# Reordering the start of a fused adaLN attention and MLP kernel: condition vector ahead of x, one PSUM bank per transposed chunk

## The chip, the cores and the metric

The kernel runs on one core of one Trainium2 chip. The metric is device time in microseconds (us) of one execution. The profile shows one execution: its span is counted from the first to the last instruction, and all times inside it are counted from the span's start. Engines: PE (matrix multiply; PEld is its weight load), DVE (vector), ACT (scalar, activations), POOL, and SP, which issues DMAs.

## The reference

One transformer block with adaptive layer norm, batch 1, 2048 tokens, width 512, 32 heads of 16, MLP width 1376, all inputs bfloat16:

```python
mod = (silu(c) @ w_mod).reshape(1, 6, 1, 512)   # c: condition vector, 512 values
sa, ca, ga, sb, cb, gb = mod[:, 0], ..., mod[:, 5]
h = layernorm(x) * (1 + ca) + sa
x = x + ga * attention(h, wqkv, wo)              # 32 heads, softmax over 2048 keys
h = layernorm(x) * (1 + cb) + sb
x = x + gb * (gelu(h @ w1 + b1) @ w2 + b2)
```

## The kernel before

The 2048 tokens are four blocks of 512 (`xb[0]` to `xb[3]`, each 4 token tiles of 128). A **prologue** handles block 0; then one long **attention stage** runs over 32 quads (a quad is four heads and one block of queries), into which the rest of the projections, the output projection and the MLP of finished blocks are woven. The order of the attention stage is written by a planner inside the kernel (jobs with due times, modelled engine clocks); the prologue is ordered by hand. The engines then run their instructions in that order, each held only by semaphores.

The prologue, by the lines that the change and the prediction touch:

- Loads. SP issues the first half of `xb[0]` (L138), ACT the second half (L138) and then the condition vector `cc_bf` (L139); each then issues half of the modulation weights `W_m0` (L128). `later_loads` (L143) puts the other loads on SP behind a trigger: a one-element memset on DVE (L145), placed behind the first statistics of block 0, into the destination of the first of these loads. The order there is W_k (first half), W_q (first half), `xb[1]`, W_v, `xb[2]`, `xb[3]` and the rest.
- `silu_c` (L196): one exponential on ACT (L198), three small operations on DVE (L199 to L201). It stands in DVE's order ahead of the layer-norm statistics of block 0 (`ln_stats`, L213, one per token tile).
- `warm_up` (L376): 18 matmuls on zeros that keep PE busy while x is loaded. Behind them `first_mod_mm` (L267): 32 matmuls of width 1 that make the modulation columns in `psm`.
- `ln1_norm` (L353): square root on ACT (L248), four normalisations on DVE (L253).
- Transposes (L258): 16 of 128x128, chunk by chunk of the width; a chunk j takes the same 128 columns of all four token tiles. Chunks 0 and 1 share one PSUM tile (a bank), chunks 2 and 3 another.
- `first_mod` (L282, L283) copies the modulation columns; `hT_evac` (L298 on DVE for chunks 0 and 2, L295 on ACT for chunks 1 and 3) scales, shifts and writes `hT`.
- `k_proj` (L303, four matmuls), `k_evac` on ACT (L309), `q_proj` (L317), then `ST1` = 3 statistics of block 1, then `q_evac` (L326): two operations on DVE that write the two halves of `qm`, for even and odd heads; the fourth statistic of block 1 is a planner's job and comes after it.

The attention stage reserves its PSUM banks after the prologue's pools are closed: two single banks `psX0`, `psX1` (name `aux`), one for the output of a quad (`od`), three for scores `sA`, two for scores `sB`. In the prologue the pools stood in the order: one bank for `psm`, two for the transposes, four for products (`ppj`), so that the query products lay in a bank that later belongs to `sA`. First in the stage come scores of quad 0 (L1019, `sA` and `sB`), two value products (L332), and the exponentials on ACT (L1071). Value products are evicted by ACT (L339). Matmuls on zeros (L1235, "fills") are put in by the planner where PE would have little to do. Layer norm of blocks 1 to 3 runs on DVE as jobs: four aggregations (L221), three small steps (L223 to L227), six newton steps (L235 to L238), four normalisations (L253); then transposes, evictions, and `k_proj` with an eviction on DVE (L311).

Of the kernel before, what the change touches and what calls it, by code (L numbers as in the profile page):

```python
# [12 lines left out]
BF16 = mybir.dt.bfloat16  # L13
FP32 = mybir.dt.float32
# [3 lines left out]
PSUM = bass.MemoryType.PSUM  # L18
DRAM = bass.MemoryType.DRAM

P = 128
# [4 lines left out]
NC = 4  # L26
# [24 lines left out]
PE_, ACT_, DVE_, POOL_, SP_ = range(5)  # L51
# [4 lines left out]
PE_LAT = 0.18  # L56
EXP = {1: 0.5, 2: 0.92, 3: 1.34}

ST1 = 3

WARM = 18

# [13 lines left out]
V_EVAC = 0.63  # L76
# [17 lines left out]
def adaln_block(ctx: ExitStack, tc: tile.TileContext, A_x, A_wqkv, A_wo, B_x, B_w1, B_b1, B_w2, B_b2,  # L94
                c, w_mod, out):
    nc = tc.nc
    x_tok = A_x[0].rearrange("(b t p) d -> b p t d", b=NQB, p=P)
# [8 lines left out]
    hT = res.tile([P, NC, S], BF16, name="hT")  # L106
# [13 lines left out]
    pron = pro.enter_context(tc.tile_pool(name="pron", bufs=2, side="right"))  # L120
# [3 lines left out]
    def load_mod(i, engs):  # L124
        t = prom.tile([P, NC, 2 * D], BF16, name="W_m")
        n = NC // len(engs)
        for k, eng in enumerate(engs):
            eng.dma_start(out=t[:, n * k:n * k + n, :], in_=wm_v[:, n * k:n * k + n, 2 * i * D:2 * (i + 1) * D])  # L128
        return t

    xb = [prox.tile([P, 4, D], BF16, name="xb") for _ in range(NQB)]
    cc_bf = const.tile([P, NC], BF16, name="cc_bf")
    W_k = prow.tile([P, NC, D], BF16, name="W_k")
    W_v = prow.tile([P, NC, D], BF16, name="W_v")

    two = (nc.sync, nc.scalar)
    for k, eng in enumerate(two):
        eng.dma_start(out=xb[0][:, 2 * k:2 * k + 2, :], in_=x_tok[0][:, 2 * k:2 * k + 2, :])  # L138
    nc.scalar.dma_start(out=cc_bf, in_=c.rearrange("o (p j) -> p (o j)", j=NC))  # L139
    W_m0 = load_mod(0, two)  # L140
    mods = {}

    def later_loads():  # L143

        nc.vector.memset(W_k[0:1, 0, 0:1], 0.0)  # L145
        nc.sync.dma_start(out=W_k[:, :, 0:256], in_=wqkv_v[:, :, D:D + 256])
        nc.sync.dma_start(out=W_q[:, :, 0:256], in_=wqkv_v[:, :, 0:256])
        nc.sync.dma_start(out=xb[1], in_=x_tok[1])
        nc.sync.dma_start(out=W_v, in_=wqkv_v[:, :, 2 * D:3 * D])
        for b in range(2, NQB):  # L150
            nc.sync.dma_start(out=xb[b], in_=x_tok[b])
        nc.sync.dma_start(out=W_k[:, :, 256:D], in_=wqkv_v[:, :, D + 256:2 * D])
        nc.sync.dma_start(out=W_q[:, :, 256:D], in_=wqkv_v[:, :, 256:D])
        mods[1] = load_mod(1, (nc.sync,))
# [4 lines left out]
    ident = const.tile([P, P], BF16, name="ident")  # L159
# [52 lines left out]
    def ln_stats(src, st, t, i):  # L212
        nc.vector.bn_stats(out=st[:, i, :], in_=src[:, t, :])  # L213
# [42 lines left out]
    def transpose_chunk(ps, src, j, tiles):  # L256
        for i, t in enumerate(tiles):
            nc.tensor.transpose(out=ps[:, i * P:(i + 1) * P], in_=src[:, t, j * P:(j + 1) * P],  # L258
                                identity=ident)
# [17 lines left out]
    def first_mod_mm(ps):  # L277
        mod_cols(ps, W_m0, 0, 0)
        mod_cols(ps, W_m0, D, 4)
# [13 lines left out]
    def hT_evac(dst, ps, col, eng):  # L293
        if eng == "act":
            nc.scalar.activation(out=dst, in_=ps, func=ACT.Identity, bias=modc[:, col:col + 1],  # L295
                                 scale=modc[:, col + 4:col + 5])
        else:
            nc.vector.tensor_scalar(out=dst, in0=ps, scalar1=modc[:, col + 4:col + 5],  # L298
                                    scalar2=modc[:, col:col + 1], op0=ALU.mult, op1=ALU.add)
# [51 lines left out]
    hn_t = [None] * NQB  # L351

    def ln1_norm(b, st):  # L353

        mv, rs = ln_sqrt(st, 4)

        nc.scalar.activation(out=ce_x, in_=eps_c, func=ACT.Exp)
        for t in range(4):
            ln_norm(xb[b], xb[b], mv, rs, t, t)
        hn_t[b] = xb[b]  # L360

    with tc.tile_pool(name="pps", bufs=1, space=PSUM) as pps0, \
            tc.tile_pool(name="ppst", bufs=2, space=PSUM) as ppst, \
            tc.tile_pool(name="ppsm", bufs=4, space=PSUM) as ppsm:
        silu_c()
        st0 = pron.tile([P, 12, 6], FP32, name="st1")
        for t in range(4):
            ln_stats(xb[0], st0, t, t)
            if t == 0:
                later_loads()  # L370

        idle = ppsm.tile([P, 512], FP32, name="ppj")

        def warm_up(n):
            for _ in range(n):
                nc.tensor.matmul(out=idle, lhsT=warm[:, 0:P], rhs=warm, start=True, stop=True)  # L376
        warm_up(WARM)
        psm = pps0.tile([P, 16], FP32, name="psm")
        ln1_norm(0, st0)
        pt_ = [ppst.tile([P, 2, 512], BF16, name="ptr") for _ in range(2)]  # L380
        first_mod_mm(psm)
        for j in range(NC):
            transpose_chunk(pt_[j // 2][:, j % 2, :], hn_t[0], j, range(4))
        first_mod(psm)
        for j in range(NC):
            hT_evac(hT[:, j, 0:512], pt_[j // 2][:, j % 2, :], j, "act" if j % 2 else "dve")
        ps = ppsm.tile([P, 512], FP32, name="ppj")
        k_proj(ps, 0, 0)
        k_evac(ps, 0, 0, "act")
        ps = ppsm.tile([P, 512], FP32, name="ppj")  # L390
        q_proj(ps, 0, 0)
        st1 = pron.tile([P, 12, 6], FP32, name="st1")
        for t in range(ST1):
            ln_stats(xb[1], st1, t, t)
        q_evac(ps, 0, 0)

# [29 lines left out]
    lab = {}  # L426
# [13 lines left out]
    def job(at, rows, needs=(), label=None, hold=-1):  # L440
        jobs.append(Job(at, rows, needs, label, hold))

    lab[("k", 0, 0)] = lab[("q", 0, 0)] = lab[("x", 0)] = 0.0
    st_of = {1: st1}
    V_ENG = ["act"] * 9 + ["dve", "act", "dve", "dve", "act", "dve", "dve"]

# [56 lines left out]
    for b in range(1, NQB):  # L503
        at = 0.25 * (b - 1)
        def stats(j, b=b, t=0):
            if b > 1 and t == 0:
                st_of[b] = pron.tile([P, 12, 6], FP32, name="st1")
            ln_stats(xb[b], st_of[b], t, t)
        job(at - 0.16, [(DVE_, V_EVAC, lambda j, b=b, t=t, f=stats: f(j, b, t)) for t in range(ST1 if b == 1 else 0, 4)],
            [("n", b - 1)] if b > 1 else [], ("st", b))  # L510
        job(at - 0.1, ln_rows(b, lambda b=b: xb[b], lambda b=b: xb[b], "n"), [("st", b)], ("n", b))
        for j in range(NC):
            h_job(at, b, j)
        k_job(at + 0.01, 0, b)
        if b == 1:
            for kt in range(4):
                v_job(0.02, kt)
# [917 lines left out]
    while pv["q"] < nq or od_copy or jobs or active:  # L1435
        q = next_quad[0] - 1
# [50 lines left out]
```

## Time and profile before

| what | value |
|---|---|
| runs | 819.32, 817.38, 819.41 us; median 819.32 |
| profiled execution | 815.8 us, span 814.0 us |
| busy share of the span | PE 95%, ACT 93%, DVE 89%, POOL 9% |
| condition vector | issued 1.26, landed 5.80 |
| first layer-norm statistics (DVE) | 6.56 |
| warm-up block on PE | 2.68 to 9.55 |
| transposes of block 0 | 10.37 to 12.24 |
| block 1 of x | issued 8.26, landed 13.46 |
| query eviction | 15.28 to 16.68 |
| first scores, first exponential | 16.82, 17.31 |

The busy shares are means over stages with different limits. In the views, a line gives the start, the length, the engine, the line of the kernel, the operation, what it writes and reads, and in brackets how long its engine sat idle before it and what ended that wait. The chain view follows the work back from the last instruction of a stretch to what released it.

### The profile page before, as it was taken

The page shows a single profiled execution, that of the slowest core. Times are in us where ns is not written, and L with a number is a line of the kernel's source. Part 1 is how long each engine was busy: PE and PEld are TensorE (multiplying, and loading weights), DVE is VectorE, ACT ScalarE, POOL GpSimd, SP SyncE. Part 2 cuts the span into 40 slices and gives each one's busy share as a digit, 9 for nine tenths or more (in the row PEclk, how much of TensorE's full clock was granted, in tenths as well). Part 3 has the DMA queues.
Part 4 walks back from the last instruction along what each step waited for, and adds up shares of the span by engine and source line. Part 5 has one row for each costly group of instructions (what it writes and reads, how often), then busy time and mean ns, then how long its engine had stood idle before and what let it go on. Part 6 is the DMA issues. An engine that isn't in the chain of part 4 may idle for free.

```text
span 814.0 us, 18164 instructions
## 1 busy us (share of the span) xinstructions
PE 771.9 (95%) x7404; PEld 237.5 (29%) x7470; DVE 723.8 (89%) x1306; ACT 756.2 (93%) x681; POOL 71.2 (9%) x62
## 2 busy tenths in 40 slices
PE   7999999989999999999999999999999999999997
PEld 3432222322223222222222322222222222222254
DVE  7879989999998998998998999988998999889663
ACT  4898999989998999999999999999999999999962
POOL 0000000024000000101100000011100000011100
PEclk9999999999999999999999999999999999999999
DMA  8100000104100000001100000010100000010100
GB/s 269 68 1 16 15 16 15 42 16 140 41 15 16 15 17 2 14 23 29 48 16 16 16 10 8 14 29 21 48 15 16 15 3 15 15 28 23 48 2 29
DMA packets 30426, 24.49 MB, mean 30 GB/s; under 512 B 13473, under 2 KB 24194, under 8 KB 30338
## 3 DMA queue, kind: packets, MB, share of 16 engines
q1 hardware_dynamic: 29650, 22.49, 9.6%
q8 instruction: 60, 0.98, 0.5%
q10 hardware_dynamic: 688, 0.79, 0.3%
q14 instruction: 28, 0.23, 0.1%
HBM read 20.65 MB, written 2.61 MB: 29 GB/s over the span
## 4 chain that ended last, share of the span: by engine, by line
PE 46%; ACT 24%; DVE 17%; issue 10%; DMA 2%; SPq 0%; POOL 0%; ACTq 0%; DVEq 0%; POOLq 0%
PE od L1214 14%; ACT pA L1071 14%; ACT pB L1071 9%; DVE t L1137 7%; PE sA L1019 6%; PE sB L1019 6%; DVE t L1158 6%; PE aux L1019 4%; PE aux L678 3%; PE od L1235 2%; PE aux L615 2%; PE aux L653 2%; PE aux L303 1%; PE fb L805 1%; PE aux L317 1%
## 5 line engine op out<-in xcount | busy, mean ns | idle before, releaser
L1071 ACT ACTIVATE pA<-sA 128x1536 bf16<-128x1536 f32 x310 | 469.1, 1513 | 16.3 <-PE od L1214 7.2
L1137 DVE TENSOR_SCALAR t<-aux 128x512 int16<-128x512 f32 x500 | 328.8, 682 | 30.6 <-PE aux L1019 29.2
L1071 ACT ACTIVATE pB<-sB 128x1024 bf16<-128x1024 f32 x309 | 336.4, 1089 | 6.3 <-PE od L1214 3.9
L1158 DVE TENSOR_SCALAR t<-t 128x2048 int16<-128x2048 int16 x375 | 260.1, 715 | 2.6 <-PE od L1214 1.4
L1019 PE MATMUL aux<-qm,kT 32*128 32x512 bf16 x500 | 177.5, 380 | 6.2 <-DVE t L1137 3.4
L1019 PEld LDWEIGHTS <-kT 32*128 32x128 bf16 x2048 | 75.9, 91 | 266.9 <-issue 262.6
L1214 PE MATMUL od<-pA,VE 128*32 128x512 bf16 x930 | 141.7, 385 | 0.6 <-DVE o_sb L1253 0.5
L1214 PE MATMUL od<-t,VV 128*32 128x512 f16 x1500 | 139.6, 385 | 1.5 <-DVE t L1158 1.2
L1214 PE MATMUL od<-pB,VE 128*32 128x512 bf16 x618 | 140.7, 385 | 0.1
L1019 PE MATMUL sA<-qm,kT 32*128 32x512 bf16 x930 | 123.0, 384 | 10.5 <-ACT pA L1071 4.7
L1019 PE MATMUL sB<-qm,kT 32*128 32x512 bf16 x618 | 121.1, 384 | 5.3 <-ACT pB L1071 2.4
L1272 POOL TENSOR_TENSOR OT<-o_sb,rb 128x512 bf16<-128x512 f32 x31 | 43.2, 1394 | 559.3 <-DMA rb<-d 288.4
L1214 PEld LDWEIGHTS <-VE 128*32 128x32 bf16 x2048 | 50.3, 94 | 95.9 <-issue 83.2
L1235 PE MATMUL od<-hT,zeros 128*32 128x512 bf16 x844 | 76.0, 385 | 0.0
L1214 PEld LDWEIGHTS <-VV 128*32 128x32 bf16 x1500 | 39.7, 95 | 58.8 <-issue 50.2
L1214 PE MATMUL od<-t,VE 128*32 128x512 f16 x500 | 49.5, 384 | 2.7 <-DVE o_sb L1253 2.7
L678 PE MATMUL aux<-W,uG 128*128 128x512 bf16 x120 | 35.5, 383 | 1.6 <-issue 1.6
L653 PE MATMUL aux<-h2T,W 128*128 128x512 bf16 x113 | 35.6, 384 | 0.5 <-issue 0.3
L1235 PEld LDWEIGHTS <-zeros 128*32 128x32 bf16 x872 | 21.8, 95 | 36.1 <-issue 30.6
L658 DVE TENSOR_SCALAR uG<-aux,b1c 128x512 bf16<-128x512 f32 x33 | 24.4, 741 | 4.8 <-PE aux L653 4.8
L615 PE MATMUL aux<-W_o_pad,OT 128*128 128x512 bf16 x88 | 25.6, 382 | 0.7 <-issue 0.5
L688 POOL TENSOR_TENSOR ob<-tmp,xr 128x512 bf16<-128x512 f32 x12 | 15.7, 1305 | 115.1 <-DVE tmp L684 115.1
(156 smaller groups left out, 430.9 us busy)
## 6 DMA issues: line engine op xcount, KB each, us to landing
rb<-d SPq DMA_DIRECT2D x124, 64.0 KB
W_m<-in_w_mod_dram SPq DMA_DIRECT2D x2, 1024.0 KB
xr<-in_A_x_dram SPq DMA_DIRECT2D x4, 512.0 KB
out_dram<-ob SPq DMA_DIRECT2D x15, 128.0 KB
xb<-in_A_x_dram SPq DMA_DIRECT2D x3, 512.0 KB
W<-in_B_w_dram SPq DMA_DIRECT2D x1, 1376.0 KB
W<-in_B_w_dram SPq DMA_DIRECT2D x1, 1280.0 KB
W_m<-in_w_mod_dram SPq DMA_DIRECT2D x1, 512.0 KB
```

What stands on the lines that cost most here:

```text
L615: nc.tensor.matmul(out=j.ps, lhsT=OT[(b, t)][:, tt * P:(tt + 1) * P], rhs=W_o_pad[:, t, :], start=False, stop=(t == 7))
L653: nc.tensor.matmul(out=j.ps, lhsT=late["W_1"][:, c, fc * P:(fc + 1) * P], rhs=T["h2"][:, c, :], start=(c == 0), stop=(c == NC - 1))
L658: nc.vector.tensor_scalar(out=T["u"][:, fc, :], in0=j.ps, scalar1=late["b1c"][:, fc:fc + 1], scalar2=None, op0=ALU.add)
L678: nc.tensor.matmul(out=j.ps, lhsT=T["u"][:, fc, tt * P:(tt + 1) * P], rhs=late["W_2"][:, fc, :], start=False, stop=(fc == NFC - 1))
L688: nc.gpsimd.tensor_tensor(out=o, in0=j.tmp, in1=T["x1"][:, tt, :], op=ALU.add)
L1019: nc.tensor.matmul(out=dst, lhsT=kT[32 * r:32 * r + 32, ch, kt * P:(kt + 1) * P], rhs=qm[(b, ch)][32 * r:32 * r + 32, par, :], start=True, ...
L1071: nc.scalar.activation(out=pt[:, 0:n, :], in_=st[:, 0:n, :], func=ACT.Exp, scale=math.log(2.0) / STEP)
L1137: nc.vector.tensor_scalar(out=t0[(qi, kt)][:, r, :], in0=sd, scalar1=T_BIAS, scalar2=0.0, op0=ALU.add, op1=ALU.max)
L1158: nc.vector.tensor_scalar(out=t16, in0=t0[(qi, kt)], scalar1=float(MJ[j]), scalar2=None, op0=ALU.add)
L1214: nc.tensor.matmul(out=od[qi][32 * r:32 * r + 32, :], lhsT=w, rhs=src, start=first, stop=last_)
L1235: nc.tensor.matmul(out=dst[32 * r:32 * r + 32, :], lhsT=zeros, rhs=hT[:, r, 0:512], start=bank is not None, stop=bank is not None)
L1272: nc.gpsimd.tensor_tensor(out=OT[(b, t)], in0=o, in1=j.rb, op=ALU.mult)
```

## The change

- ACT issues the condition vector ahead of its half of `xb[0]`.
- Behind the trigger, which now is a memset into `xb[1]`, `xb[1]` is loaded first, then W_k, W_q, W_v as before.
- The PSUM pools of the prologue stand in another order and size: three banks for products, four for the transposes, one for `psm`. Each transposed chunk has a bank of its own, and the query products lie in a bank that is not one of the later score banks.
- The transposes go token tile by token tile (all four chunks of a tile), no longer chunk by chunk.
- One statistic of block 1 stands behind the normalisations of block 0 and ahead of the modulation copies; the other three stand ahead of the query eviction. The planner's job for the remaining one is gone, and the label that it would have set is given from the start.

```diff
-ST1 = 3
+ST1 = 1
...
     two = (nc.sync, nc.scalar)
+    nc.scalar.dma_start(out=cc_bf, in_=c.rearrange("o (p j) -> p (o j)", j=NC))
     for k, eng in enumerate(two):
         eng.dma_start(out=xb[0][:, 2 * k:2 * k + 2, :], in_=x_tok[0][:, 2 * k:2 * k + 2, :])
-    nc.scalar.dma_start(out=cc_bf, in_=c.rearrange("o (p j) -> p (o j)", j=NC))
     W_m0 = load_mod(0, two)
...
     def later_loads():
-        nc.vector.memset(W_k[0:1, 0, 0:1], 0.0)
+        nc.vector.memset(xb[1][0:1, 0, 0:1], 0.0)
+        nc.sync.dma_start(out=xb[1], in_=x_tok[1])
         nc.sync.dma_start(out=W_k[:, :, 0:256], in_=wqkv_v[:, :, D:D + 256])
         nc.sync.dma_start(out=W_q[:, :, 0:256], in_=wqkv_v[:, :, 0:256])
-        nc.sync.dma_start(out=xb[1], in_=x_tok[1])
         nc.sync.dma_start(out=W_v, in_=wqkv_v[:, :, 2 * D:3 * D])
...
-    with tc.tile_pool(name="pps", bufs=1, space=PSUM) as pps0, \
-            tc.tile_pool(name="ppst", bufs=2, space=PSUM) as ppst, \
-            tc.tile_pool(name="ppsm", bufs=4, space=PSUM) as ppsm:
+    with tc.tile_pool(name="ppsm", bufs=3, space=PSUM) as ppsm, \
+            tc.tile_pool(name="ppst", bufs=4, space=PSUM) as ppst, \
+            tc.tile_pool(name="pps", bufs=1, space=PSUM) as pps0:
...
         ln1_norm(0, st0)
-        pt_ = [ppst.tile([P, 2, 512], BF16, name="ptr") for _ in range(2)]
+        st1 = pron.tile([P, 12, 6], FP32, name="st1")
+        for t in range(ST1):
+            ln_stats(xb[1], st1, t, t)
+        pt_ = [ppst.tile([P, 512], BF16, name="ptr") for _ in range(NC)]
         first_mod_mm(psm)
-        for j in range(NC):
-            transpose_chunk(pt_[j // 2][:, j % 2, :], hn_t[0], j, range(4))
+        for t in range(4):
+            for j in range(NC):
+                nc.tensor.transpose(out=pt_[j][:, t * P:(t + 1) * P], in_=xb[0][:, t, j * P:(j + 1) * P],
+                                    identity=ident)
         first_mod(psm)
         for j in range(NC):
-            hT_evac(hT[:, j, 0:512], pt_[j // 2][:, j % 2, :], j, "act" if j % 2 else "dve")
+            hT_evac(hT[:, j, 0:512], pt_[j], j, "act" if j % 2 else "dve")
...
         q_proj(ps, 0, 0)
-        st1 = pron.tile([P, 12, 6], FP32, name="st1")
-        for t in range(ST1):
+        for t in range(ST1, 4):
             ln_stats(xb[1], st1, t, t)
         q_evac(ps, 0, 0)
...
-    lab[("k", 0, 0)] = lab[("q", 0, 0)] = lab[("x", 0)] = 0.0
+    lab[("k", 0, 0)] = lab[("q", 0, 0)] = lab[("st", 1)] = lab[("x", 0)] = 0.0
...
-        job(at - 0.16, [(DVE_, V_EVAC, ...) for t in range(ST1 if b == 1 else 0, 4)],
-            [("n", b - 1)] if b > 1 else [], ("st", b))
+        if b > 1:
+            job(at - 0.16, [(DVE_, V_EVAC, ...) for t in range(4)],
+                [("n", b - 1)], ("st", b))
```

More of the change, by code (lines that the diff above doesn't have):

```diff
@@ L505, in stats @@
         def stats(j, b=b, t=0):
-            if b > 1 and t == 0:
+            if t == 0:
                 st_of[b] = pron.tile([P, 12, 6], FP32, name="st1")
             ln_stats(xb[b], st_of[b], t, t)
-        job(at - 0.16, [(DVE_, V_EVAC, lambda j, b=b, t=t, f=stats: f(j, b, t)) for t in range(ST1 if b == 1 else 0, 4)],
-            [("n", b - 1)] if b > 1 else [], ("st", b))
+        if b > 1:
+            job(at - 0.16, [(DVE_, V_EVAC, lambda j, b=b, t=t, f=stats: f(j, b, t)) for t in range(4)],
+                [("n", b - 1)], ("st", b))
         job(at - 0.1, ln_rows(b, lambda b=b: xb[b], lambda b=b: xb[b], "n"), [("st", b)], ("n", b))
```

## The prediction

> **What bounds the kernel now.** I read the page first. ACT, PE and DVE are all over 88% busy across the span, coupled in one hand-planned order, so a change confined to the start can only move the moment at which that coupled stage begins.
>
> ```profile
> span 814.0 us, 18164 instructions
> ...
> PE 771.9 (95%) x7404; PEld 237.5 (29%) x7470; DVE 723.8 (89%) x1306; ACT 756.2 (93%) x681; POOL 71.2 (9%) x62
> ```
>
> Next, the chain that ended last, taken over the first 30 us (start, length, what), shows what sets that moment:
>
> ```profile
> 1.26 4.54 DMA cc_bf<-in_c_dram
> ...
> 6.64 0.64 DVE st L213 x2
> ...
> 8.26 5.20 DMA xb<-in_A_x_dram
> ...
> 13.49 1.88 DVE st L213 x3
> 15.37 1.31 DVE qm L326 x2
> ...
> 17.31 1.45 ACT pA L1071
> ```
>
> The condition vector lands at 5.80 and holds DVE, which runs in order, away from the first statistics; the second block of x is issued at 8.26 and lands at 13.46; the first exponential starts at 17.31. The time-ordered view gives the pieces between (start, length, engine):
>
> ```profile
> 2.68 6.87 PE L376 MATMUL ppj<-warm 128*128 128x512 bf16 x18 [2.68 <-DVE warm L184]
> 9.39 0.94 PE L267 MATMUL psm<-sc_bf,W_m 128*128 128x1 bf16 x32
> 9.90 1.38 DVE L253 TENSOR_SCALAR xb<-xb,mv,rs 128x512 bf16<-128x512 bf16 x4
> 10.37 1.87 PE L258 MATMUL ptr<-ident,xb 128*128 128x128 bf16 x16
> 11.83 1.00 DVE L298 TENSOR_SCALAR hT<-ptr,modc 128x512 bf16<-128x512 bf16 x2 [0.41 <-PE ptr L258]
> 12.41 1.45 ACT L295 ACTIVATE hT<-ptr,modc 128x512 bf16<-128x512 bf16 x2 [1.25 <-DVE hT L298]
> 15.28 1.40 DVE L326 TENSOR_SCALAR qm<-ppj,qmask 128x512 bf16<-128x512 f32 x2
> 16.82 0.39 PE L1019 MATMUL sA<-qm,kT 32*128 32x512 bf16 x3 [1.67 <-DVE qm L326]
> ```
>
> Warm-up, modulation columns and transposes stand behind each other on PE without a gap. ACT's two evictions of the transposed chunks sat 1.25 us idle behind DVE's, and the first scores 1.67 us behind both halves of the query products.
>
> **Which instructions move.** In the order of the two built programs only the first 30 us differ: statistics, the newton steps of the next block and one pack of 8 zero matmuls move or go; from there on every engine has the same sequence. So the sum is the shift at the start, carried to the end.
>
> **Condition vector first.** ACT issues it at 0.75 instead of 1.26, ahead of its half of x. Its landing lies between 3.6 (ACT's table load ends at 2.30 + 1.28 = 3.58, nothing earlier helps) and 0.75 + 4.54 = 5.29, if it were as slow as before. That slowness was half of x in the same queue ahead of it, so I take 3.9. The row 5.83 to 6.56 puts the first statistics 0.73 later: 4.63, a gain of 1.93 for the whole layer-norm chain. The four normalisations then run 7.97 to 9.35. ACT's half of x goes out 0.5 later; it had landed before the vector did, within 5.05 of its issue, hence by 6.31 now, against the third statistics at 4.63 + 2 x 0.62 = 5.87. Value: no stall; worst: 0.44, which the next part covers.
>
> Here is a page that speaks against this edit: the Trainium skill, "DMA: Bandwidth & Descriptors", Bandwidth, says that small transfers are dominated by their descriptors (under 64 KB). Its table has 0.68 us for 4 KB, so by it an estimated 0.7 us of queue time goes ahead of x, and the sum would not change, being under the cover just named. No row here times the 1 KB alone.
>
> **PE becomes the bound, so most of that is not passed on.** The warm-up block is unchanged, so the 32 modulation matmuls still end at 10.33, and the transposes start at 10.37 as before. What goes are the waits on the normalisations: the last 13 transposes took 0.90 to 12.24, 57 ns apart with 219 for the last. Sixteen at 57 ns, by token tile, put the last tile into chunk 0 (13th) at 10.37 + 12 x 0.057 + 0.22 = 11.27, into chunk 1 at 11.33. In chunk order chunk 1 would have been ready at 10.99, so the new order gives away 0.34 here; it pays only where the normalisations are late.
>
> **A bank per chunk.** Before, chunk 0 had to wait for chunk 1's transposes in the same tile, and ACT for DVE's read. Now ACT's evictions start at 11.37 instead of 12.41: 1.04 gained. ACT's pair (1.45) is longer than DVE's (1.00), so key products, key eviction and query products all come 1.04 earlier; the last query product ends at 14.11 instead of 15.15.
>
> **Statistics of block 1.** The block is now first behind the trigger, issued at about 5.37 (trigger behind the first statistics, 0.1 later, as 7.19 to 7.30). Before, data moved 1.3 us after the 7.30 issue, and the queue then ran at 273 to 288 GB/s; 512 KB make 1.9, so it lands at about 8.6, I take 9.4 for a slow DMA engine. One statistic (0.68) now stands on DVE ahead of the modulation copies (0.27): 9.4 + 0.65 + 0.3 gives 10.4, hidden up to 11.27. At the row's 5.20 us from issue to landing it would be 10.57, and 0.3 late. The other three take 12.25 to 14.12, just under the query products. W_k and W_q go out 0.5 later behind x in SP's queue, but 1.4 earlier in time; at 0.9 per 256 KB behind 9.4 they land by 10.3 and 11.2, needed at 11.9 and 13. W_v and the later blocks keep their bytes ahead and start 1.9 sooner.
>
> **Query products.** The eviction starts at 14.17 instead of 15.28. The first scores now wait for the first half alone: 14.17 + 0.74 + 0.14 (16.68 to 16.82 before) = 15.05, and the first exponential starts 0.49 later, at 15.5 instead of 17.31: 1.8 gained. The second half holds the first value product to 15.7, PE being free at 15.45; that ends at 16.7, while ACT is in its first exponential to 16.95. Cover 0.25.
>
> **The next key block.** The second stall is at 28.86, scores waiting for the next keys (ACT idle 2.26 up to 28.42). Shifted by 1.8, DVE has the fourth statistic of block 2 ahead of the evictions (ends 21.45, needed 21.47), then aggregate and three steps (1.01) ahead of the other two evictions: 23.4, 0.2 late. But only six newton steps and one normalisation (1.16 + 0.36) then stand ahead of the key copy: 24.3 + 1.5 = 25.8, end 26.5, scores at 26.65: 2.2 before 28.86. Without the 8 zero matmuls (0.55 ahead of the scores at 28.31) PE is free at 26.4. So 2.2 is what reaches the common sequence.
>
> **The clock gate.** This sum uses the profiled warm-up. Its weight loads are 0.43 us apart until 8.20 and about 0.2 after 8.5: the array runs at half pace for 5.8 us from 2.68. The windows show the length of one closed stretch (PE, PEld, DVE, ACT, POOL busy, granted clock, DMA):
>
> ```profile
> 172.50:175.90 3.40, 2.22 (x23) 0.43 (x20) 3.40 (x6) 2.15 (x3) 0.24 (x1) 0.97 0.00 0
> 175.90:179.30 3.40, 3.04 (x20) 0.51 (x17) 2.99 (x5) 2.02 (x3) 0.00 (x0) 0.53 0.00 0
> 179.30:182.70 3.40, 3.40 (x44) 1.09 (x47) 3.18 (x6) 3.40 (x3) 0.72 (x3) 1.00 0.27 40
> ```
>
> One stretch of 3.4 us. If opening goes by the same grid, with a phase that the kernel does not set, it comes one to two such stretches after the first matmul, 3.4 to 6.8, middle 5.1; the profiled 5.8 is late. Each microsecond sooner saves 0.5 on the warm-up. Before, this was hidden by the normalisations to 11.28; after, PE's path is the bound and takes it, down to the floor of DVE's path (10.45 instead of 11.31). So the gain is 1.7 to 3.0 by phase, in the middle 2.2 + 0.7 x 0.5 = 2.55. The Trainium skill, "TensorE: Matmul & The Clock Gate", Part 1: The HAM clock gate, has the window as 3413 ns and free-running, not reset at a kernel's start; the closed stretch agrees, and by the page the time would be in the same 1.7 to 3.0; that the phase differs from run to run one trace cannot show.
>
> **The number.** The profiled execution took 815.8, 1.8 more than its span; the same sum there gives 815.8 - 2.2 = 813.6. The runs shown have a median of 819.32, 3.5 above it. I take the shift from that: 819.32 - 2.55 = 816.8. A measurement of this kernel can tell about 0.3% (2.5 us) from no change, and the forecast lies on that edge.
>
> **Rivals.**
> 1. One closed stretch fewer than in the timed runs of before. Price: ACT idled twice for 1.25 to 1.38 in and around the one in the trace, and PE's half pace loses 1.7; I take 1.6. For it: the trace has a single one after an idle PE (1.18 us), and the timed runs lie 1.6 to 3.6 above it. Against: nothing there is edited. Time 815.2.
> 2. The first part does not do what it says: block 1 or W_k lands late, or the vector at 5.29. Price 0.4 to 1.5 of the gain; against it stand the covers above. Time 818.3.
> 3. Slower: the gate closes oftener. Eight keep-busy matmuls are gone and all later work lies elsewhere on the grid. Two closings more cost 3.2 and turn the gain into 816.8 + 3.2 = 820.0; from the second on it is slower than before, from the fourth by over 0.3%. Against it: PE's idle stretches at the start shrink (1.67 to 0.9 ahead of the first scores).
>
> **Chances.** Forecast 0.72 (own range 815.9 to 818.0 with the scatter of a median; 0.45 of it beyond 0.3%, 0.27 within); rival 1 0.12, faster; rival 2 0.09, within; rival 3 0.07, of which 0.05 slower by over 0.3% and 0.02 within. Faster 0.57, same 0.38, slower 0.05. The range from 814.6 to 819.0 takes in rivals 1 and 2 and the floor of the phase, and leaves rival 3 out.
>
> **What would show it.** In the changed profile: vector landed by about 4, first statistics near 4.6, normalisations done near 9.4 while PE is still in the warm-up or modulation; no idle time of PE between transposes; ACT's evictions straight behind them, not behind DVE; first scores 0.14 behind the first half of the query products; first exponential at 14.7 to 15.9; scores on the second key block near 26.6; the same order and the same stage lengths after that. It is wrong if the normalisations still gate the transposes, if block 1 lands after 10.3, or if the span after the first 30 us changes by more than a closed stretch.

## The result, and the profile after

The changed kernel took 815.89 us in the median of 15 runs (812.40 to 817.65), beside 819.08 for 15 runs of the kernel before (816.16 to 821.26). The ratio is 0.9962, 95% interval 0.9948 to 0.9977: 3.2 us less, 1.9 to 4.3 by the interval. A second set, listed below, gave 0.9952 (0.9927 to 0.9976). The profiled execution took 815.01; the page shows hardly more than that every engine has the same work as before:

```profile
span 813.1 us, 18148 instructions
...
PE 770.4 (95%) x7396; PEld 238.1 (29%) x7462; DVE 724.8 (89%) x1306; ACT 756.4 (93%) x681; POOL 70.3 (9%) x62
```

The chain that ended last, taken over the first 30 us (start, length, what), shows a new hold-up. The condition vector is gone from it, and block 1 of x has moved forward to hold the statistic, the modulation columns and the evictions (here and below, lines between those shown are left out, and line numbers are those of each run's own kernel):

```profile
4.32 0.64 DVE st L213 x2
...
4.97 5.00 DMA xb<-in_A_x_dram
...
9.99 0.70 DVE st L213
10.69 0.06 DVE modc L282
10.75 0.08 DVE modc L283
...
10.92 1.00 DVE hT L298 x2
11.92 1.78 DVE st L213 x3
13.70 1.41 DVE qm L326 x2
```

The time-ordered view of the same stretch (in brackets the idle time and what ended it):

```profile
2.67 6.13 PE L376 MATMUL ppj<-warm 128*128 128x512 bf16 x18 [2.67 <-DVE warm L184]
4.24 1.30 DVE L213 BATCH_NORM_STATS2 st<-xb 128x6 f32<-128x512 bf16 x2
7.58 1.38 DVE L253 TENSOR_SCALAR xb<-xb,mv,rs 128x512 bf16<-128x512 bf16 x4
8.64 0.94 PE L267 MATMUL psm<-sc_bf,W_m 128*128 128x1 bf16 x32
9.44 1.05 PE L387 MATMUL ptr<-ident,xb 128*128 128x128 bf16 x16
9.99 0.70 DVE L213 BATCH_NORM_STATS2 st<-xb 128x6 f32<-128x512 bf16 x1 [1.03 <-DMA xb<-in_A_x_dram]
10.92 1.45 ACT L295 ACTIVATE hT<-ptr,modc 128x512 bf16<-128x512 bf16 x2 [2.07 <-DVE modc L283]
13.69 1.41 DVE L326 TENSOR_SCALAR qm<-ppj,qmask 128x512 bf16<-128x512 f32 x2
14.49 0.39 PE L1024 MATMUL sA<-qm,kT 32*128 32x512 bf16 x3 [0.84 <-DVE qm L326]
14.98 1.45 ACT L1076 ACTIVATE pA<-sA 128x1536 bf16<-128x1536 f32 x1 [1.57 <-PE sA L1024]
```

Normalisations end at 8.96 instead of 11.28, under the cover of the warm-up and the modulation matmuls. PE goes through these and the transposes without a gap, to 10.49. Both evictions start together at 10.92, where ACT had started at 12.41, but 0.43 behind the last transpose: DVE had waited 1.03 for block 1. The first exponential starts at 14.98 instead of 17.31: 2.33 sooner. The second key block follows. Before:

```profile
28.86 0.39 PE L1019 MATMUL sA<-qm,kT 32*128 32x512 bf16 x3
...
29.30 1.45 ACT L1071 ACTIVATE pA<-sA 128x1536 bf16<-128x1536 f32 x1 [0.29 <-PE sA L1019]
```

After:

```profile
25.98 0.54 PE L1024 MATMUL sA<-qm,kT 32*128 32x512 bf16 x3
...
26.57 1.46 ACT L1076 ACTIVATE pA<-sA 128x1536 bf16<-128x1536 f32 x1
```

From there the exponentials stay between 2.6 and 2.9 ahead of their times before, up to 170 us. Then the clock gate takes most of the difference between these two executions: the kernel before had one closed stretch at 175.9, the kernel after two in a row, in the row of windows (PE, PEld, DVE, ACT, POOL busy, granted clock, DMA):

```profile
198.50:201.90 3.40, 1.86 (x23) 0.62 (x22) 3.40 (x3) 2.32 (x2) 2.48 (x2) 0.94 0.02 2
201.90:205.30 3.40, 3.24 (x23) 0.52 (x23) 3.17 (x7) 1.45 (x1) 0.00 (x0) 0.50 0.02 2
205.30:208.70 3.40, 3.40 (x35) 0.72 (x27) 2.39 (x5) 2.67 (x3) 0.00 (x0) 0.56 0.28 76
```

A quiet PE (1.86 of 3.40), then two stretches at half clock. So the profiled pair differs by only 0.8, and the medians say more than the pair.

### The profile page after: what moved, and what is told of

It reads as the page before. It is cut to its first block, busy times and chain, and to the rows that moved or that the text cites. A ratio compares the mean times of both kernels' runs of the same rounds, so it can differ in the third digit from the quotient of the medians.

```text
span 813.1 us, 18148 instructions
## 1 busy us (share of the span) xinstructions
PE 770.4 (95%) x7396; PEld 238.1 (29%) x7462; DVE 724.8 (89%) x1306; ACT 756.4 (93%) x681; POOL 70.3 (9%) x62
## 4 chain that ended last, share of the span: by engine, by line
PE 48%; ACT 26%; DVE 15%; issue 10%; DMA 1%; POOL 0%; SPq 0%; ACTq 0%; POOLq 0%; DVEq 0%
PE od L1219 15%; ACT pA L1076 14%; ACT pB L1076 9%; PE sA L1024 7%; PE sB L1024 6%; DVE t L1142 5%; DVE t L1163 5%; PE aux L1024 4%; PE od L1240 3%; PE aux L683 3%; PE aux L620 2%; PE aux L303 1%; PE fb L810 1%; PE aux L658 1%; PE aux L332 1%
```

## Experiments

Theory at the outset: the gain is the shift of the first exponential, made by the early condition vector, a bank of its own for each transposed chunk and query products outside the score banks; block 1's landing is the new bound. Rivals: the parts do not do this, or the gain is a matter of how often the gate closes. Four kernels in a first set, four in a second, four in a third; the kernel before had medians of 817.68, 817.81 and 818.09 in them. Each ratio is to the kernel before in the same set, with its 95% interval. The forecasts also call DVE VectorE and ACT ScalarE.

### The condition vector alone (in the kernel before)

```diff
+    nc.scalar.dma_start(out=cc_bf, in_=c.rearrange("o (p j) -> p (o j)", j=NC))
     for k, eng in enumerate(two):
...
-    nc.scalar.dma_start(out=cc_bf, in_=c.rearrange("o (p j) -> p (o j)", j=NC))
```

> The kernel before with one part of the change alone: the condition vector issued ahead of ACT's half of x. My theory (the layer-norm chain gains 2.3 us, but PE's warm-up and modulation block then sets the start): the normalisations end near 9.0, the transposes follow the modulation matmuls without a wait, ACT's eviction starts 1.3 us behind the end of the modulation matmuls (chunk 1 shares a bank with chunk 0, then DVE's read goes first), and the first exponential comes 4.9 us behind that eviction: 15.8 to 16.5, by the phase of the clock gate, so 0.8 to 1.5 of the 2.33 us that the whole change gained there. Rival (the vector was hidden, all gain is in the banks): first exponential at 17.2 to 17.4 as before.

817.84 us (8 runs), ratio 0.996 (0.9929 to 0.9992). Its profile, time-ordered:

```profile
10.26 0.99 DVE L298 TENSOR_SCALAR hT<-ptr,modc 128x512 bf16<-128x512 bf16 x2 [0.24 <-PE ptr L258]
10.84 1.44 ACT L295 ACTIVATE hT<-ptr,modc 128x512 bf16<-128x512 bf16 x2 [1.98 <-DVE hT L298]
12.69 1.88 DVE L213 BATCH_NORM_STATS2 st<-xb 128x6 f32<-128x512 bf16 x3 [1.43 <-DMA xb<-in_A_x_dram]
14.48 1.39 DVE L326 TENSOR_SCALAR qm<-ppj,qmask 128x512 bf16<-128x512 f32 x2
16.51 1.45 ACT L1071 ACTIVATE pA<-sA 128x1536 bf16<-128x1536 f32 x1 [3.18 <-DVE st L213]
```

The transposes now run without waits (9.62 to 10.67), but ACT still starts behind DVE (the shared bank), and the query eviction stands behind three statistics that wait 1.43 for block 1, which was issued at 5.94, behind W_k and W_q. Of 2.3 us gained at the norms, 0.8 are left at the first exponential, which at 16.51 lies at the late end of the forecast. In this execution the clock gate then closed from 17.5 to 20.9, and the second key block's exponential came at 29.76, 0.46 later than before. The first step is right; what it is worth alone, this profile can't say, and the runs below put it at 0.7 +- 0.8.

### The query products' bank alone: two attempts

The first attempt put the pools in the changed order but kept four product banks.

```diff
-    with tc.tile_pool(name="pps", bufs=1, space=PSUM) as pps0, \
+    with tc.tile_pool(name="ppsm", bufs=4, space=PSUM) as ppsm, \
             tc.tile_pool(name="ppst", bufs=2, space=PSUM) as ppst, \
-            tc.tile_pool(name="ppsm", bufs=4, space=PSUM) as ppsm:
+            tc.tile_pool(name="pps", bufs=1, space=PSUM) as pps0:
```

> The kernel before with another part alone: the order of the prologue's PSUM pools, so that the query products lie outside the banks of the first scores; sizes and everything else as before. My theory: the first scores start 0.14 us behind the first half of the query eviction, 0.74 sooner, first exponential at 16.5 to 16.65, whatever the phase of the clock gate, since the normalisations hide PE's block here. Rival (the scores waited for the second half of qm or for DVE's order, not for the bank): first exponential at 17.2 to 17.4.

819.73 us (8 runs), ratio 1.0008 (0.9982 to 1.0035): the expectation failed, because the edit did not do what it was meant to. The first scores still waited for the second half of the eviction (from 15.96; first exponential at 17.98, 2.02 behind). By the order of the pools the fourth product bank still lies where a score bank is later. It serves as a run without effect. The second attempt has three product banks, as the change has, and takes this wait away (against the first attempt):

```diff
-    with tc.tile_pool(name="ppsm", bufs=4, space=PSUM) as ppsm, \
+    with tc.tile_pool(name="ppsm", bufs=3, space=PSUM) as ppsm, \
```

> The kernel before with the three banks for products allocated first, two for transposes, the modulation's last: the first scores then share no bank with the query's product that is evicted by its second half; nothing else of the change is in it. If the bank does what the prediction counted (one half of the query's eviction, 0.70, off the way to the first scores): first scores start 0.1 to 0.2 behind the end of the first half of the eviction, first exponential 1.3 to 1.4 behind the eviction's start where it was 2.0 to 2.1, time 0.4 to 0.8 us less if the gain lasts. If not: the first exponential still follows the start of the query's eviction by 2.0 to 2.1, and the time is the same within 0.3%.

816.60 us (10 runs), ratio 0.9983 (0.9965 to 1.0001).

```profile
14.20 1.88 DVE L213 BATCH_NORM_STATS2 st<-xb 128x6 f32<-128x512 bf16 x3 [1.38 <-DMA xb<-in_A_x_dram]
15.99 1.39 DVE L326 TENSOR_SCALAR qm<-ppj,qmask 128x512 bf16<-128x512 f32 x2
16.78 0.39 PE L1019 MATMUL sA<-qm,kT 32*128 32x512 bf16 x3 [1.64 <-DVE qm L326]
17.28 1.45 ACT L1071 ACTIVATE pA<-sA 128x1536 bf16<-128x1536 f32 x1 [2.38 <-PE sA L1019]
```

The mechanism is as forecast: first exponential 1.29 behind the start of the eviction, where it was 2.03 in the kernel before. In this execution block 1 came late (statistics at 14.20 against 13.49), so the exponential is no sooner than before. The time agrees with 0.4 to 0.8 less as it does with none.

### Transposes in chunk order (in the changed kernel)

```diff
-        for t in range(4):
-            for j in range(NC):
+        for j in range(NC):
+            for t in range(4):
                 nc.tensor.transpose(out=pt_[j][:, t * P:(t + 1) * P], in_=xb[0][:, t, j * P:(j + 1) * P],
                                     identity=ident)
```

> The changed kernel with the transposes in the order of before, chunk by chunk, each still in its own bank. My theory: the evictions wait for the modulation copies behind the statistic of block 1 (DMA of block 1 lands at about 10.0), so the order of the transposes does not matter: ACT's eviction at 10.9, first exponential 14.9 to 15.0, unless the modulation matmuls end later than 9.9, when chunk order is up to 0.3 us sooner than token order would be. Rival (the order by token tile is what frees the evictions): evictions 0.3 us or more later than in the changed kernel, first exponential 15.3 or later.

815.64 us (8 runs), ratio 0.9982 (0.9965 to 0.9998). The transposes took 1.05 either way, and what followed did not hang on their order:

```profile
10.49 0.69 DVE L213 BATCH_NORM_STATS2 st<-xb 128x6 f32<-128x512 bf16 x1 [1.53 <-DMA xb<-in_A_x_dram]
```

The gate opened early here: the warm-up block, whose matmuls run 0.43 us apart before the opening and 0.22 after it, was 5.76 long, against 6.13. The transposes were done at 10.13, and the evictions still began only at 11.42, behind block 1. PE idled, and two closed stretches followed:

```profile
10.00:11.70 1.70, 0.13 (x3) 0.10 (x1) 1.10 (x4) 0.28 (x1) 0.00 (x0) 1.00 1.05 347
...
13.40:16.80 3.40, 2.56 (x10) 0.52 (x8) 2.40 (x8) 0.68 (x2) 0.00 (x0) 0.50 1.13 348
16.80:20.20 3.40, 3.40 (x12) 1.04 (x11) 3.06 (x16) 2.65 (x3) 0.00 (x0) 0.56 1.05 393
```

They run from 13.0 to 19.8; the first exponential is at 16.71 instead of 14.98, and that of the second key block at 29.74, later than before. An early opening bought nothing here, because the bound was not PE. That the idle time brought the closing is likely, not shown: in the next run PE was busy for 0.03 of the 1.70 us from 9.7, and the clock stayed at 1.00.

### Without the early statistic (in the changed kernel; three sets)

```diff
-        for t in range(ST1):
-            ln_stats(xb[1], st1, t, t)
...
-        for t in range(ST1, 4):
+        for t in range(3):
             ln_stats(xb[1], st1, t, t)
         q_evac(ps, 0, 0)
+        ln_stats(xb[1], st1, 3, 3)
```

> The changed kernel without the statistic of block 1 ahead of the modulation copies: three statistics ahead of the query eviction, the fourth right behind it. My theory (that statistic waits for block 1's DMA and holds the modulation copies, and so the evictions): the copies follow the modulation matmuls at once, ACT's eviction starts about 1.05 us behind the end of the modulation matmuls (transposes), 10.6 for the phase of the clock gate seen so far instead of 10.92, first exponential 0.3 us sooner, 14.7; with a late gate no difference. The fourth statistic (0.65) now stands in DVE's chain to the second key block, which takes back up to 0.2 there. Rival (the key weights' DMA, landed at 10.86, is as late, or the DMA of block 1 holds the next statistics and so the query eviction): first exponential unchanged at 14.9 to 15.0.

812.35 us (3 runs), ratio 0.9919 (0.9888 to 0.995). In this profile the gate opened earliest of all (warm-up 5.36 long); then W_k is last to come:

```profile
9.66 1.45 ACT L295 ACTIVATE hT<-ptr,modc 128x512 bf16<-128x512 bf16 x2 [0.81 <-PE ptr L385]
11.48 1.04 PE L303 MATMUL ppj<-hT,W_k 128*128 128x512 bf16 x4 [1.75 <-DMA W_k<-in_A_wqkv_dram]
```

Such a low time asked for a repeat, beside the changed kernel itself.

> The changed kernel once more, beside the others of this set. If the time between the first matmul and the end of the evictions is set by when block 1 of x and W_k land, and that differs from run to run (issue to landing 5.0 us for block 1 in the first profile of this kernel, 5.5 with the transposes in chunk order), then this profile shows again an idle stretch of VectorE ahead of the early statistic, of 0.5 to 1.6 us, and evictions that start 0.9 us behind the landing. If the first profile was a chance, the statistic starts behind its norms (end 8.96) without idle time. Time: 0.994 to 0.998 of the kernel before in both.

814.67 us (5 runs), ratio 0.9952 (0.9927 to 0.9976), with the same wait in the profile: statistic at 10.04 after 1.08 idle for block 1, evictions at 10.97, first exponential 15.03. But here the gate opened later (warm-up 6.52), the transposes ended at 10.89, behind the modulation copies (10.86), and ACT was released by them:

```profile
10.96 1.45 ACT L295 ACTIVATE hT<-ptr,modc 128x512 bf16<-128x512 bf16 x2 [2.12 <-PE ptr L387]
```

So the two chains, block 1 through DVE and the transposes through PE, end within 0.1 of each other in this execution, and the late block 1 cost next to nothing. This execution took 818.39, 3.4 more than the first profile of the same kernel, though its prologue was as far ahead: the gate closed again near 271 and 458.

> The changed kernel with no statistic of block 1 ahead of the copies of the modulation (three ahead of the query's eviction, one behind). It gave 812.35 in three runs, 3.3 under the others of its set with a low count. Theory 1 (the early statistic makes VectorE, and with it both evictions, wait for block 1): evictions start 0.2 to 0.3 behind the last transpose, W_k (issue to landing 5 to 6 us) is then the last to come and the first key product starts at 10.9 to 11.5; first exponential 14.6 to 15.0 against 15.0 to 16.7 with the early statistic, time 0.5 to 1.5 us under the changed kernel. Theory 2 (the low time was a chance of the clock gate): the same start of the evictions, but time within 0.5 us of the changed kernel.

812.86 us (4 runs), ratio 0.9936 (0.9913 to 0.9958). The evictions start at 10.49 and 10.54, about 0.1 ahead of the end of the transposes (10.61), with nothing else to hold them:

```profile
9.56 1.05 PE L385 MATMUL ptr<-ident,xb 128*128 128x128 bf16 x16
...
10.54 1.45 ACT L295 ACTIVATE hT<-ptr,modc 128x512 bf16<-128x512 bf16 x2 [1.70 <-PE ptr L385]
```

The first exponential is at 14.61, 0.4 ahead of the changed kernel.

> The changed kernel without the early statistic a third time, in more rounds, since seven runs of it lay between 811.7 and 813.8. Theory 1 (the early statistic costs by its wait for block 1, 0.3 to 1 us, and the rest of the low time was the chance of where the clock gate closes): ratio to the kernel before 0.9945 to 0.996, 0.5 to 1.5 us under the changed kernel's 0.9962. Theory 2 (it is better by some 2.5 to 3 us, so something beyond the first 15 us must have changed with it): ratio 0.992 to 0.994 again.

814.29 us (9 runs), ratio 0.996 (0.9936 to 0.9983), first exponential at 15.05 with a late gate (warm-up 6.69). The 0.992 to 0.994 of theory 2 did not come again, so a good part of the low times was chance. That the early statistic waits for block 1 is shown by the profiles; that leaving it out gains in time is not: the intervals of all sets overlap.

### What holds block 1 and W_k back?

Two trials on the kernel without the early statistic. First, W_k and W_q on ACT's queue, beside block 1 on SP's:

```diff
-        nc.sync.dma_start(out=W_k[:, :, 0:256], in_=wqkv_v[:, :, D:D + 256])
-        nc.sync.dma_start(out=W_q[:, :, 0:256], in_=wqkv_v[:, :, 0:256])
...
         silu_c()
+        nc.scalar.dma_start(out=W_k[:, :, 0:256], in_=wqkv_v[:, :, D:D + 256])
+        nc.scalar.dma_start(out=W_q[:, :, 0:256], in_=wqkv_v[:, :, 0:256])
```

> As the kernel without the early statistic, and the first halves of W_k and W_q issued on ScalarE's queue right behind the exponential of the condition vector, beside block 1 on SP's queue. Theory 1 (landings of block 1 and W_k bound this stretch, because they follow each other on one queue): issued at 3.7 to 5.0, W_k lands at 8.5 to 9.5, so no wait for W_k is left; key products start 0.7 to 0.8 behind the start of the evictions (10.3 to 10.6 where the modulation ends at 8.7 to 9.6), first exponential at 13.5 to 14.3, 0.5 to 1.2 ahead of the kernel without the early statistic, time less by 0.4 to 1.0 us. Rival (all queues share the same 16 DMA engines, so an earlier weight delays the second half of the modulation weights or block 1 by what it gains): modulation products start later than 8.64 or the three statistics of block 1 wait past 12, first exponential not before 14.7, time within 0.4 us of it.

814.85 us (10 runs), ratio 0.9962 (0.9944 to 0.9979). No wait for W_k, issued at 3.17, is left: key products at 11.64, 0.60 behind DVE's eviction (11.04); but the repeat without the new queue had the same 0.60. First exponential 15.16 and time read like the rival's, but a late gate (warm-up 6.79) would give the same 15.16, so this trial decides only that no large gain is there.

Second, W_v and all loads behind it held until block 0 is normalized:

```diff
+    def last_loads():
+        nc.vector.memset(W_v[0:1, 0, 0:1], 0.0)
         nc.sync.dma_start(out=W_v, in_=wqkv_v[:, :, 2 * D:3 * D])
...
         ln1_norm(0, st0)
+        last_loads()
```

> As the kernel without the early statistic, and W_v, with all loads behind it, issued only when block 0 is normalized (a write of one element of W_v by VectorE behind the norms). Theory 1 (block 1 and W_k take 5 to 6 us from issue to landing because W_v and the blocks behind them, issued within 2 us, share the same 16 DMA engines): the three statistics never wait, the key products start 0.5 to 0.6 behind the start of the evictions in every profile with no wait for W_k, W_k landing by 9.5; first exponential 4.0 to 4.1 behind ScalarE's eviction (13.7 to 15.1 by the gate's opening), time 0 to 1 us less than without the hold. Rival (the transfers are bound by themselves or by the modulation weights ahead of them): W_k still lands at 10.5 to 11.4, same first exponential as without the hold, and W_v later than 14 costs up to 1 us.

815.14 us (10 runs), ratio 0.9963 (0.9943 to 0.9982).

```profile
11.69 0.55 PEld L306 LDWEIGHTS <-W_k 128*128 128x128 bf16 x4 [1.08 <-DMA W_k<-in_A_wqkv_dram]
```

W_k, issued at 5.38, still came at about 11.6 in this execution, though W_v was not issued before 9.01. Without the hold it came at 11.0 to 11.5, so W_v and the loads behind it are not what delays it. Theory 1 falls on this; the rival, which forecast 10.5 to 11.4, is the nearer one.

### The order of the loads, and the late condition vector

W_k and W_q ahead of block 1 again, on the kernel without the early statistic:

```diff
-        nc.vector.memset(xb[1][0:1, 0, 0:1], 0.0)
-        nc.sync.dma_start(out=xb[1], in_=x_tok[1])
+        nc.vector.memset(W_k[0:1, 0, 0:1], 0.0)
         nc.sync.dma_start(out=W_k[:, :, 0:256], in_=wqkv_v[:, :, D:D + 256])
         nc.sync.dma_start(out=W_q[:, :, 0:256], in_=wqkv_v[:, :, 0:256])
+        nc.sync.dma_start(out=xb[1], in_=x_tok[1])
```

> As the kernel without the early statistic, but with W_k and W_q issued ahead of block 1, in the order of the kernel before. Theory (who is issued second lands last, and the query's eviction stands behind three statistics of block 1): W_k lands by 9.7 to 10.3, block 1 at 11.0 to 12.7, statistics end 12.9 to 14.5, the query's eviction starts there, first exponential 14.2 to 16.0; time 0 to 1.5 us more than with block 1 first. Rival (the order of the loads makes no difference, both land together): first exponential 14.6 to 14.8, same time.

813.57 us (9 runs), ratio 0.994 (0.9923 to 0.9957).

```profile
12.25 1.88 DVE L213 BATCH_NORM_STATS2 st<-xb 128x6 f32<-128x512 bf16 x3 [0.87 <-DMA xb<-in_A_x_dram]
```

As expected, the wait moves from W_k to block 1: query eviction at 14.05, first exponential at 15.32, inside the forecast 14.2 to 16.0. The time is no worse, so the order of these loads is not what the gain rests on.

The condition vector behind x again, all else as changed:

```diff
-    nc.scalar.dma_start(out=cc_bf, in_=c.rearrange("o (p j) -> p (o j)", j=NC))
     for k, eng in enumerate(two):
         eng.dma_start(out=xb[0][:, 2 * k:2 * k + 2, :], in_=x_tok[0][:, 2 * k:2 * k + 2, :])
+    nc.scalar.dma_start(out=cc_bf, in_=c.rearrange("o (p j) -> p (o j)", j=NC))
```

> The changed kernel with the condition vector's load behind those of x again, as in the kernel before; all else as changed. If the early condition vector is what moves the prologue (theory of the prediction): the vector lands at 5.6 to 5.8, the first statistics start at 6.4 to 6.6, norms end 11.1 to 11.3, evictions at 11.5, first exponential 15.5 to 16.0, time 0.5 to 1.2 us more than the changed kernel; block 1, issued 2 us later, lands at 12 or later and would put the early statistic and both evictions behind it: then first exponential 16.5 to 17, and 1.5 to 2 us more. Rival (the gate and block 1's landing set the evictions whatever the vector does): first exponential at 15.0 to 15.5, time within 0.5 us.

814.72 us (9 runs, 814.29 to 817.00), ratio 0.9961 (0.9947 to 0.9974).

```profile
5.55 0.20 ACT L198 ACTIVATE ce<-cc_bf 128x4 f32<-128x4 bf16 x1 [1.97 <-DMA cc_bf<-in_c_dram]
12.14 1.45 ACT L295 ACTIVATE hT<-ptr,modc 128x512 bf16<-128x512 bf16 x2 [1.24 <-DVE modc L283]
17.43 1.45 ACT L1076 ACTIVATE pA<-sA 128x1536 bf16<-128x1536 f32 x1 [2.41 <-PE sA L1024]
```

The profile does as the theory said and goes beyond its range: late vector, norms end at 11.01, evictions at 12.14, and the first exponential at 17.43, here with a closed stretch from 13.0 to 16.4; the second key block's exponential comes at 29.02, only 0.28 sooner than before. The time does not follow: it is that of the changed kernel. Against the 0.9962 and 0.9952 of that kernel the intervals leave room for a loss of some 1.3 us, so 0.5 to 1.2 is not excluded, while 1.5 to 2 is hardly compatible. One of the nine executions was profiled (815.84 us, above the median), so how far ahead the others were is not known.

### All runs at the same clock

Each run's time has a mean granted clock beside it. Over the 182 runs that have it listed (the 15 of the kernel before in the first measurement have not), one level for each kernel and one slope common to all gives 0.51 us for each 0.001 of clock. At the same clock the kernels stand, against the kernel before (mean clock 0.9939):

| kernel | runs | mean clock | us at the same clock, 95% |
|---|---|---|---|
| changed | 20 | 0.9936 | -2.9 +- 0.5 |
| changed, no early statistic | 16 | 0.9953 | -3.6 +- 0.6 |
| the same, W_k and W_q first | 9 | 0.9960 | -3.4 +- 0.8 |
| the same, W_k and W_q on ACT's queue | 10 | 0.9938 | -3.6 +- 0.7 |
| the same, W_v held | 10 | 0.9945 | -2.9 +- 0.7 |
| changed, vector behind x | 9 | 0.9950 | -2.5 +- 0.7 |
| changed, chunk order | 8 | 0.9948 | -2.2 +- 0.8 |
| before, vector first | 8 | 0.9935 | -0.7 +- 0.8 |
| before, query bank | 10 | 0.9963 | -0.3 +- 0.7 |
| before, pool order with four banks | 8 | 0.9924 | +0.5 +- 0.8 |

The sets ran on different chips; with a level for each set as well, the changed kernel stands at -2.8 +- 1.0 and the other rows move by at most 0.3. Two things follow. The mean clock is the same before and after (0.9939, 0.9936), so the gain does not come from fewer closings. And the parts do not add: the vector alone and the query bank alone make about 1.1 together, yet no part that was undone alone takes more than 0.8 off the 2.9 in the middle of its interval. Two chains side by side, block 1 through DVE and the transposes through PE, would give such a picture: freeing one leaves the other. That is argued; the second profile of the changed kernel, where both chains end within 0.1, fits it. Which combination carries the 2.9 was not isolated: neither the bank for each chunk nor the bank of the query products was undone alone in the changed kernel.

Whether a lead at the start reaches the end at all can be read from the fourteen profiles. For each, take how far the second key block's exponential is ahead of the 29.30 of before, and how many closed stretches follow it. Before has 0 and one (span 814.0 us), changed 2.73 and two (813.1), its second profile 2.68 and four (816.5), vector behind x 0.28 and two (814.0), chunk order -0.45 and one (815.4). A straight line through all fourteen gives a span 1.2 +- 0.3 us shorter for each us of lead and 1.4 +- 0.3 longer for each closed stretch, with 0.7 us of scatter. So the lead is carried to the end about one for one, which is the step from the prologue to the time. In the runs with chunk order and with the vector behind x the profiled execution had no such lead (-0.45, 0.28), while the runs are 2.2 and 2.5 faster: one profile does not speak for its runs.

## Why the prediction was right, and where it was not

**The size.** Forecast 816.8, 2.5 less than the 819.32 of the runs shown; measured 815.89, 3.2 less than the 819.08 beside it, at the lower edge of the forecast's own range (815.9). The shift in the first 30 us, 2.33 at the first exponential and 2.73 at the second key block, stands beside the 1.7 to 3.0 of the text and the 2.9 at the same clock. The choice to carry that shift over to the runs, and not to take the difference of two profiles, was right: the pair of profiles shows 0.8. Of the signs that were named, one did not come: the evictions were not straight behind the transposes.

**Condition vector: right on the times, not on its weight.** Statistics at 4.24 against 4.63 forecast; ACT read the vector at 3.50, straight behind its table load, which is the lower bound that the text named. The whole chain of norms came 2.3 sooner, and ACT's half of x was in time, though issued 0.46 later: the four statistics ran from 4.24 to 6.72 without a wait. That most of this is not passed on, as the text said, is borne out further than it went: with the vector behind x the time at the same clock is 0.4 higher, within the uncertainty of none, and alone it gave 0.7 +- 0.8.

**"PE becomes the bound": the step that failed in part.** PE ran without gaps, and would have been the bound; but block 1 landed at 9.97, not 9.4, and the statistic in front of the modulation copies held both evictions to 10.92, 0.43 behind the end of the transposes. The term mis-sized is the landing: 5.00 us from issue, and 5.5 in the chunk-order run, against the 4.0 taken. The sum worked with a queue that starts empty. That was true before (the windows of before show 0 GB/s from 7 to 8, just ahead of the load); after, the load is issued at 4.97 while the loads ahead of it still move (399 GB/s from 5 to 6). The 5.20 of the one row at hand, named as the other end, was the better value. That it gave "0.3 late", and 0.43 was measured, is partly luck: the load went out 0.40 sooner than forecast, and the transposes ended 0.8 sooner. With the warm-up of this profile, 0.74 shorter, the sum of the text puts the evictions at 10.63 and the first exponential at 14.80; 10.92 and 14.98 came, so the late block took about 0.3 from the start. With the warm-up of before the same landing would have been hidden, and in the second profile (warm-up 6.52) it cost 0.1, PE being the bound as forecast. What failed is the gain from an early opening: the text let it go down to 10.45, but the three profiles with early vector and early statistic start their evictions at 10.92, 10.96 and 11.42 where the warm-up took 6.13, 6.52 and 5.76.

**Token order: no gain, and the loss hidden only with the early statistic.** In the first profile of the changed kernel the evictions wait for block 1, not for the last tile. Without the early statistic DVE idles 0.52 for the transposes in the repeats, so there the 0.34 given away may be lost; chunk order was not run in that kernel.

**Bank for each chunk.** DVE's and ACT's evictions start together at 10.92; with shared banks ACT starts 0.58 later, in the kernel before as in the run with the vector alone. The 1.04 was this and the transposes' waits together; 1.49 came, with 0.74 of shorter warm-up gained and the wait for block 1 lost in it.

**Query products: right.** First scores 0.80 behind the start of the eviction, 0.88 forecast; the exponential 0.49 behind them; confirmed alone by the three-bank run (0.79 and 0.50).

**Second key block: right in its added gain.** 0.4 more than the first exponential's shift was forecast, 0.40 came in the exponentials (2.33 to 2.73); the scores came at 25.98 against 26.65.

**The gate.** The warm-up's length over fourteen profiles runs from 5.36 to 6.90. Its matmuls start 0.427 us apart before the opening and 0.216 after it; read from their starts, the opening came 2.7 to 5.8 us after the first matmul. The forecast's spread of one stretch (3.4) is about right, but its place, 3.4 to 6.8, is about a microsecond late: the profiled 5.8 of before was not just late, it was at the end. So the term "0.7 x 0.5" for an earlier opening was too small (with the middle at 4.2 it is 0.8), and the late block 1 took part of that back; that the two nearly cancel is luck. The Trainium skill ("TensorE: Matmul & The Clock Gate", Part 1: The HAM clock gate) has the window free-running and not reset at a kernel's start; that the opening moves by 3.1 us behind the same warm-up agrees.

**Rivals.** The first (fewer closings) and the third (more) fall by the equal mean clock. For the first, a count agrees: the changed kernel's two profiles have two and four closed stretches, the one of before has one. A stretch cost 1.4 by the line above, against the 1.6 taken. The second came true in part: block 1 landed late, and the evictions started 0.43, 0.07 and 1.29 behind the transposes in the three profiles named above, against the 0.4 to 1.5 of the text. W_k was late too (10.86), but hidden behind the evictions.

## What to carry to other kernels

Where a load is moved forward, ask what its queue and engines are doing at the new moment: a landing time worked out from an empty queue is too short, and the whole issue-to-landing of the nearest row is the safer value. In a prologue with several chains of nearly the same length, expect little from freeing one alone: here the parts tried alone gave 0.7 and 0.3, within their uncertainty of none. Look twice at an instruction that waits for a load and stands in front of one that others wait for; the profiles show its wait here, though the runs do not show its price. When a gate that the kernel does not control moves single runs by more than the effect, compare medians at the same clock, and use a profile for the mechanism only.

## What was not expected of the hardware

- An early opening of the gate need not help: in the chunk-order run PE was busy 0.13 of 1.70 us from 10.0 to 11.7, and two stretches at 0.50 and 0.56 followed. It was not so each time: with the earliest opening (warm-up 5.36) PE idled as long, and no closing followed. The clock that is shown for the warm-up itself is 1.00 although its matmuls run at half pace (0.43 us apart).
- W_k, 256 KB, took 6.3 us from issue to the first weight load that it releases (5.38 to 11.69) with only W_q (5.94) issued behind it before 9.01. What sets that is open: the DMA engines were busy 0.87 to 0.99 from 7 to 9, at 268 to 297 GB/s, where they had moved about 400 from 4 to 6.
